# A kernel ordered by a planner: other DMA landings, margins and plays in the plan of attention with two gated layers

## The chip, the cores and the metric

The kernel runs on one core of a Trainium2 chip. The metric is the device time of one execution in microseconds; less is better. Beside the runs that were only timed there is one execution that the hardware profiler recorded, and every row below comes from that one.

## What is computed

Attention in chunks of 64 tokens (8 heads of 64, 4608 tokens), and then two layers on the 4608 x 512 result, the first with 1536 inner columns, the second with 2048. All is float32.

```python
scores = scale * np.matmul(q_c, k_c.transpose(0, 1, 2, 4, 3))
attn = np.exp(scores - np.max(scores, axis=-1, keepdims=True))
attn = attn / (np.sum(attn, axis=-1, keepdims=True) + 1e-09)
x = np.matmul(attn, v_c)                       # then as 4608 x 512
g = x @ w_gate
x = (g * (1.0 / (1.0 + np.exp(-g))) * (x @ w_val)) @ moe_w_out
h = x @ w_in
out = (h * (1.0 / (1.0 + np.exp(-1.702 * h)))) @ moe2_w_out
```

## The kernel before

**The work.** The tokens are cut into 9 blocks of 512 and the inner columns of each layer into two halves, so that there are four passes over the blocks: passes 0 and 1 for the first layer, 2 and 3 for the second. In pass 0 the attention of the next block is made between the products of the present one. Large products are made by a scheme of seven products of halves in place of eight (the labels 1 to 7), and each operand stands as a high and a low part, so that a product is three matmuls (L368 to L370, in `mm3`). A pass keeps its weights in SBUF; the tokens' combinations `x`, the output weights `o` and partial sums go through DRAM and come back by DMA.

**Weights of the next pass.** While a pass runs, the weights of the next one are prepared. `conv_tile` loads half a tile at a time into `raw` (two buffers, 255.8 KB each, L424) and `conv_part` takes it apart with two instructions on ACT (L447, L449) and two on DVE (L452, L455). POOL then makes the combinations and their low parts (L361, tiles `st` and `ws`), and SP stores them to DRAM (L348).

**The engines' queues.** Every engine works through its own list in order. All DMAs are issued by SP (L345 loads, L348 stores), so one that waits for its data holds up those behind it. ACT also copies products out of PSUM (`u<-ga`, L352, in `copy`), which sets the bank `ga` free for PE's next product.

**The planner.** The kernel lists its operations with a cost in us, the tiles they read and write, and a due time written by hand (`prio`); `Program` then sets the order in which they are written to the engines' lists, and only that order reaches the chip. `order` (L114) is a list scheduler: it lets each engine take, among the operations that are ready within a short window, the one with the earliest due time. For a DMA it supposes 1.5 us to the start, 0.865 of the cost for the transfer, behind the transfers before it, and 1.3 us to the landing. An operation of PE counts as ready `SLACK` (0.5 us) after its last operand, unless it brings a margin `near` of its own. `dues` (L160) works back from the end to the time by which each operation is due; `replay` (L186) plays the four engines and the DMA queue with the order fixed, with a model of PE's clock, and gives the time at the end. `emit` (L236) does this 12 times, each time with the due times halfway between the old and those of `dues`, and keeps the order whose replay ends first. `op` (L87) collects the dependencies; a tile that takes the place of an older one in its ring waits for the users of the older one that were listed by then (L98).

Of the kernel before, what the change touches and what calls it, by code (L numbers as in the profile page):

```python
# [2 lines left out]

# [24 lines left out]
class Buf:  # L28
# [2 lines left out]

    def __init__(self, make, prev=None, before=None, whole=None):
        self.make, self.prev, self.before, self.whole, self.bank = make, prev, before, whole, False
        self.users, self.writers, self.tile = [], [], None

    @property
    def ap(self):
# [15 lines left out]
class Ring:  # L53
# [5 lines left out]
    def new(self, shape, dtype=F32):  # L59
        def make():  # L60
            return self.pool.tile(shape, dtype, tag=self.tag, name=self.tag, bufs=self.bufs)

        prev = self.made[-self.bufs] if len(self.made) >= self.bufs else None
        b = Buf(make, prev, self.made[-1] if self.made else None)
        b.bank = self.pool is self.banks
        self.made.append(b)
        return b

# [6 lines left out]
class Program:  # L75
    HOP = {("pe", "dve"): 0.32, ("pe", "act"): 0.32, ("pe", "dma"): 0.3}
    WINDOW = {"pe": 0.3, "dve": 0.1, "act": 0.3, "pool": 0.3, "dma": 0.0}
    FREE = {"pe": 1.3, "pool": 0.7, "dma": 0.7, "act": 0.0, "dve": 0.0}
    SLACK = 0.5
    LOAD = 1.28  # L80
    ROUNDS = 12
    BEAT = 3.413
# [4 lines left out]
    def op(self, eng, us, fn, reads=(), writes=(), prio=0, table=None, near=None, port=None):  # L87
        o = Op()
        o.eng, o.us, o.fn, o.prio, o.table, o.near, o.n = eng, us, fn, prio, table, near, len(self.ops)
        o.port = eng == "pool" or eng == "dve" and port is not False and not any(a.bank for b in reads for a in b.line())  # L90
        deps, follows = set(), set()
        for b in reads:
            deps.update(next((a.writers for a in b.line() if a.writers), ()))
        for b in writes:
            deps.update(b.users)
            if not b.users:
                if b.prev is not None:
                    deps.update(b.prev.users)  # L98
                if b.before is not None and b.before.tile is None:
                    follows.add(b.before.users[0])  # L100
        for b in (*reads, *writes):
            for a in b.line():
                a.users.append(o)
        for b in writes:
            for a in b.line():
                a.writers.append(o)
        o.deps, o.follows = deps, follows - deps
        self.ops.append(o)
        return o
# [4 lines left out]
    def order(self):  # L114
        ready = {eng: [] for eng in self.FREE}
        for o in self.ops:
            o.ready, o.left = 0.0, len(o.deps) + len(o.follows)
            if not o.left:
                ready[o.eng].append(o)
        free, table, port, moved, seq = dict(self.FREE), None, 0.0, 0.0, []  # L120
        while len(seq) < len(self.ops):
            pick = None
            for eng, todo in ready.items():
                if not todo:
                    continue
                t = free[eng]
                limit = min(max(t, o.ready) for o in todo) + self.WINDOW[eng]
                o = min((o for o in todo if o.ready <= limit), key=lambda o: (o.key, o.n))
                s = max(t, o.ready)
                if pick is None or s < pick[0]:  # L130
                    pick = s, o
            s, o = pick
            ready[o.eng].remove(o)
            o.begin = s
            if o.eng == "dma":
                free["dma"] = s + 0.47
                moved = max(s + 1.5, moved) + 0.865 * o.us
                o.end = moved + 1.3
            else:
                if o.table and o.table != table:  # L140
                    s, table = s + self.LOAD, o.table
                if o.port:
                    o.end = max(s + 0.1, port) + o.us - 0.1
                    port = o.end - 0.1
                else:
                    o.end = s + o.us
                free[o.eng] = o.end - (0.05 if o.eng != "pe" else 0.0)
            seq.append(o)
            for a in o.after:
                if o in a.deps:  # L150
                    late = self.hop(o, a)
                    if a.eng == "pe" != o.eng:
                        late += self.SLACK if a.near is None else a.near
                    a.ready = max(a.ready, o.end + late)
                a.left -= 1
                if not a.left:
                    ready[a.eng].append(a)
        return seq

    def dues(self, seq):  # L160
        last = max(o.end for o in seq)
        for o in seq:
            o.left = len(o.after)
        heap = [(-o.end, -o.n, o) for o in seq if not o.left]
        heapq.heapify(heap)
        free = last
        while heap:
            o = heapq.heappop(heap)[2]
            t = last
            for a in o.after:  # L170
                if o not in a.deps:
                    t = min(t, a.due)
                else:
                    t = min(t, a.due - self.hop(o, a) - (self.SLACK if a.eng == "pe" != o.eng else 0.0))
            if o.eng == "dma":
                o.due = t - 2.8 - 0.865 * o.us
            elif o.eng == "pe":
                o.due = free = min(t, free) - o.us
            else:
                o.due = t - o.us  # L180
            for d in (*o.deps, *o.follows):
                d.left -= 1
                if not d.left:
                    heapq.heappush(heap, (-d.end, -d.n, d))

    def replay(self, seq):  # L186
        queue = {eng: [] for eng in self.FREE}
        for o in reversed(seq):
            queue[o.eng].append(o)
            o.end = None  # L190
        free, table, port, moved = dict(self.FREE), None, 0.0, 0.0
        busy, clock, beat = {}, 0.5, 0
        left, last = len(seq), 0.0
        while left:
            pick = None
            for eng, todo in queue.items():
                if not todo or any(d.end is None for d in todo[-1].deps):
                    continue
                o = todo[-1]
                s = max([free[eng], *(d.end + self.hop(d, o) for d in o.deps)])  # L200
                if pick is None or s < pick[0]:
                    pick = s, o
            s, o = pick
            queue[o.eng].pop()
            left -= 1
            us = o.us
            if o.eng == "dma":
                free["dma"] = s + 0.47
                moved = max(s + 1.5, moved) + 0.865 * us
                o.end = moved + 1.3  # L210
                continue
            if o.eng == "pe":
                while beat < s // self.BEAT:
                    share = busy.get(beat, 0.0) / self.BEAT
                    clock = 1.0 if share > 0.85 else 0.5 if share < 0.5 else clock
                    beat += 1
                if clock < 1.0 and us < 3.0:
                    us *= 1.8
                t = s
                while t < s + us:  # L220
                    k = t // self.BEAT
                    e = min(s + us, (k + 1) * self.BEAT)
                    busy[k] = busy.get(k, 0.0) + e - t
                    t = e + 1e-9
            if o.table and o.table != table:
                s, table = s + self.LOAD, o.table
            if o.port:
                o.end = max(s + 0.1, port) + us - 0.1
                port = o.end - 0.1
            else:  # L230
                o.end = s + us
            free[o.eng] = o.end - (0.05 if o.eng != "pe" else 0.0)
            last = max(last, o.end)
        return last

    def emit(self):  # L236
# [6 lines left out]
        for i in range(self.ROUNDS):  # L243
            seq = self.order()
            self.dues(seq)
            last = self.replay(seq)
            if best is None or last < best[0]:
                best = last, seq
            for o in self.ops:
                if o.prio < 9999:  # L250
                    o.key = (o.key + o.due) / 2
# [5 lines left out]
def attention_two_moe_kernel(ctx: ExitStack, tc: tile.TileContext, q, k, v, wg, wv, wo, wi, wo2, out):  # L257
# [38 lines left out]
    UPB = BT // P  # L296
# [744 lines left out]
    for p, (layer, gs) in enumerate(passes):  # L1041
        jobs = spread(p)
        for b in range(NB):
            t = start[p][b]
            xs = X.pop((p, b))
            for j, g in enumerate(gs):
# [62 lines left out]
                if p == 0 and b + 1 < NB:  # L1109
                    units = range(2 if b > 1 else 0, UPB + 2 if b else UPB)  # L1110
                    for u in units[len(units) * j // len(gs):len(units) * (j + 1) // len(gs)]:
                        if b:
                            attend_next(UPB * (b + 1) + u, t + -6.0 + (u - 2) * 13.5)
                        else:
                            attend(UPB + u, t + 4 + u * 16, t - 6 + u * 16)
                    if end:
# [54 lines left out]
```

## Time and profile before

| what | us |
|---|---|
| median of 3 runs | 1768.72 (1765.05 to 1769.85) |
| the profiled execution | 1770.99 |
| its span, from the first to the last instruction | 1769.2 |
| PE, matmuls busy in the span | 1704.2 |
| DVE, ACT, POOL busy | 1134.3, 888.1, 728.6 |

The span is read by engine and by stage. PE is the tensor engine's matmuls and PEld its weight loads, which run beside them; a matmul's end is modelled, so the idle time of PE comes out shorter than that of PEld. A wait is put down to what came last before the instruction could start. SPq is SP's queue of DMA issues.

### The profile page before, as it was taken

Reading aid. Unit: us, or ns where it says so; the run is one execution under the profiler, and the core shown is the slowest. Engines: PE = TensorE matmul, PEld = TensorE weight load, DVE = VectorE, ACT = ScalarE, POOL = GpSimd, SP = SyncE. Lnnn points to the kernel's source line nnn. Section 1 sums busy time; section 2 is a strip of 40 time slices with the busy share of each in tenths; the row PEclk is TensorE's granted clock in tenths of the full one; section 3 lists DMA queues with packets and bytes.
Section 4 is the critical chain, followed back from the end, with each engine's and each line's share of the span. In section 5 each row is a group of like instructions: output and inputs, shape, how many; then the busy total and the mean of one; then the engine's idle time right before and its main releaser. Section 6 shows DMA issues by size and latency. Waiting matters only on the chain.

```text
span 1769.2 us, 36486 instructions
## 1 busy us (share of the span) xinstructions
PE 1704.2 (96%) x14392; PEld 1618.5 (91%) x14392; DVE 1134.3 (64%) x1632; ACT 888.1 (50%) x1537; POOL 728.6 (41%) x762
## 2 busy tenths in 40 slices
PE   6899999999999999999999989999999999999998
PEld 6788889889889999999999889999999999999998
DVE  7887787778774345455444457777655556666656
ACT  6777666767653233333333345555544444444443
POOL 5754476666674011222212234757621133333333
PEclk7899999999999999999999999999999999999999
DMA  7468888888879767777778978988877977777783
GB/s 262 162 236 287 300 307 305 264 321 310 274 258 393 279 216 247 239 248 248 257 246 307 403 251 290 297 307 305 300 229 270 379 235 246 249 225 236 227 261 127
DMA packets 187323, 477.91 MB, mean 270 GB/s; under 512 B 20112, under 2 KB 47760, under 8 KB 187152
## 3 DMA queue, kind: packets, MB, share of 16 engines
q1 hardware_dynamic: 187152, 475.58, 78.2%
q8 instruction: 114, 1.87, 0.4%
q14 instruction: 57, 0.47, 0.1%
HBM read 334.46 MB, written 141.03 MB: 269 GB/s over the span
## 4 chain that ended last, share of the span: by engine, by line
PE 67%; DMA 13%; DVE 7%; POOL 5%; issue 4%; ACT 3%; SPq 0%; POOLq 0%; DVEq 0%; ACTq 0%
PE ga L368 8%; PE ga L370 8%; PE ga L369 8%; PE ya L368 4%; PE ya L370 4%; PE yb L368 4%; PE ya L369 4%; PE yb L370 3%; PE yb L369 3%; PE gb L368 3%; PE gb L370 3%; PE gb L369 3%; DMA raw<-in_moe_w_out 2%; PE s L368 2%; PE s L370 2%
## 5 line engine op out<-in xcount | busy, mean ns | idle before, releaser
L368 PE MATMUL ga<-x,w 128*128 128x256 f32 x1640 | 470.0, 287 | 20.9 <-ACT u L352 13.4
L369 PE MATMUL ga<-x,w 128*128 128x256 f32 x1640 | 464.6, 283 | 1.7 <-DVE x L361 1.7
L370 PE MATMUL ga<-x,w 128*128 128x256 f32 x1640 | 465.1, 284 | 0.7 <-POOL w L361 0.7
L368 PEld LDWEIGHTS ga<-x,w 128*128 128x128 f32 x1640 | 312.1, 190 | 37.0 <-ACT u L352 19.6
L369 PEld LDWEIGHTS ga<-x,w 128*128 128x128 f32 x1640 | 311.5, 190 | 7.7 <-DVE x L361 2.2
L370 PEld LDWEIGHTS ga<-x,w 128*128 128x128 f32 x1640 | 311.6, 190 | 0.9 <-POOL w L361 0.9
L352 ACT COPY u<-ga 128x512 f32<-128x512 f32 x231 | 134.7, 583 | 202.0 <-PE ga L370 201.6
L361 DVE TENSOR_TENSOR c<-u,ga 128x512 f32<-128x512 f32 x143 | 97.8, 684 | 129.7 <-PE ga L370 114.6
L361 POOL TENSOR_TENSOR k<-xr,q 128x512 fp32r<-128x512 f32 x24 | 34.3, 1427 | 329.1 <-DVE c L361 233.6
L361 DVE TENSOR_TENSOR c<-u,gb 128x512 f32<-128x512 f32 x125 | 85.3, 682 | 118.2 <-ACT u L352 103.2
L828 ACT ACTIVATE xr<-c 128x512 f32<-128x512 f32 x140 | 88.3, 631 | 142.0 <-DVE c L361 127.1
L368 PE MATMUL gb<-x,w 128*128 128x256 f32 x500 | 144.7, 289 | 7.1 <-DVE c L361 5.1
L369 PE MATMUL gb<-x,w 128*128 128x256 f32 x500 | 142.9, 286 | 3.1 <-POOL x L361 3.1
L370 PE MATMUL gb<-x,w 128*128 128x256 f32 x500 | 142.8, 286 | 0.0
L361 DVE TENSOR_TENSOR xr<-xr 128x512 f32<-128x512 f32 x140 | 123.3, 881 | 17.2 <-ACT xr L828 12.3
L788 ACT ACTIVATE h<-c 128x512 f32<-128x512 f32 x108 | 67.8, 631 | 102.7 <-DVE c L361 100.4
L361 DVE TENSOR_TENSOR h<-h,c 128x512 f32<-128x512 f32 x108 | 98.5, 920 | 27.4 <-ACT h L788 26.0
L361 POOL TENSOR_TENSOR u<-u 128x512 f32<-128x512 f32 x36 | 47.4, 1316 | 158.5 <-ACT u L352 158.5
L368 PEld LDWEIGHTS gb<-x,w 128*128 128x128 f32 x500 | 96.3, 193 | 12.6 <-DVE c L361 7.0
L447 ACT ACTIVATE t<-raw,offset 128x256 f32<-128x256 int16 x120 | 63.0, 527 | 87.4 <-DMA raw<-in_moe_w_out 31.1
L452 DVE SCALAR_TENSOR_TENSOR t<-t,raw 128x256 int32<-128x256 f32 x120 | 74.6, 628 | 48.0 <-ACT raw L449 41.7
L369 PEld LDWEIGHTS gb<-x,w 128*128 128x128 f32 x500 | 96.2, 192 | 6.7 <-POOL x L361 3.4
(252 smaller groups left out, 5003.4 us busy)
## 6 DMA issues: line engine op xcount, KB each, us to landing
x<-x_dram SPq DMA_DIRECT2D x189, 512.0 KB, 5.4
o<-od_b SPq DMA_DIRECT2D x119, 512.0 KB, 4.5
o<-od_a SPq DMA_DIRECT2D x102, 512.0 KB, 5.3
x_dram<-x SPq DMA_DIRECT2D x63, 512.0 KB, 5.3
wd_b<-ws SPq DMA_DIRECT2D x56, 256.0 KB, 4.2
od_b<-ws SPq DMA_DIRECT2D x56, 256.0 KB, 4.5
w<-wd_b SPq DMA_DIRECT2D x28, 512.0 KB, 6.4
raw<-in_moe_w_out SPq DMA_DIRECT2D x56, 255.8 KB, 4.2
```

What stands on the lines that cost most here:

```text
L352: op("act", act_us(n), lambda: nc.scalar.copy(out=dst.ap, in_=cut(src.ap)), [src], [dst], prio, near=near)
L361: lambda: e.tensor_tensor(out=dst.ap, in0=of_a(a.ap), in1=of_b(b.ap), op=by), [a, b], [dst], prio, near=near)
L368: nc.tensor.matmul(o, ah, bh, start=first, stop=False, **kind)
L369: nc.tensor.matmul(o, ah, bl, start=False, stop=False, **kind)
L370: nc.tensor.matmul(o, al, bh, start=False, stop=last, **kind)
L447: op("act", conv_us(n), lambda: nc.scalar.activation(out=t.ap, in_=raw.ap[:, :, 2], func=AF.Relu, scale=up, bias=offset.ap[:, :1]), [raw, ...
L452: op("dve", dve_us(n), lambda: nc.vector.scalar_tensor_tensor(out=t.ap.bitcast(I32), in0=t.ap, scalar=-4096 * up, in1=word(1).bitcast(F32) ...
L788: op("act", act_us(512), lambda h=h, i=i: nc.scalar.activation(out=h.ap, in_=of(0)(c[i].ap), func=AF.Silu), [c[i]], [h], prio, "silu")
L828: op("act", act_us(512), lambda: nc.scalar.activation(out=h.ap, in_=c.ap, func=AF.Gelu_apprx_sigmoid), [c], [h], prio, "gelu")
```

## The change

No instruction of the kernel is added or taken away; what is changed is what the planner supposes, and so the order of each engine's list.

- The landing of a DMA is supposed later: 0.95 of the cost in place of 0.865, and 2.4 us behind it in place of 1.3 (`LAND`). In the replay the part behind the transfer is 1.4 us with a scatter drawn anew for every DMA, and the time of an order is the mean of three such plays.
- `SLACK` goes from 0.5 to 0.3 us. Each step back from one operation to the one it needs takes 0.3 us more (`DUE`), and a DMA is due earlier by 0.7 us and the longer transfer.
- A tile that opens a reused place in a ring now depends on all users of the older tile, those listed later too (`openers`, `next`).
- The attention of blocks 2 and on gets other due times (L1113).

```diff
--- before.py
+++ after.py
@@ -1,4 +1,5 @@
 import heapq
+import random
 from contextlib import ExitStack
 
 import concourse.bass as bass
@@ -31,7 +32,7 @@
 
     def __init__(self, make, prev=None, before=None, whole=None):
         self.make, self.prev, self.before, self.whole, self.bank = make, prev, before, whole, False
-        self.users, self.writers, self.tile = [], [], None
+        self.users, self.writers, self.openers, self.next, self.tile = [], [], [], None, None
 
     @property
     def ap(self):
@@ -63,6 +64,8 @@
         prev = self.made[-self.bufs] if len(self.made) >= self.bufs else None
         b = Buf(make, prev, self.made[-1] if self.made else None)
         b.bank = self.pool is self.banks
+        if prev is not None:
+            prev.next = b
         self.made.append(b)
         return b
 
@@ -76,7 +79,9 @@
     HOP = {("pe", "dve"): 0.32, ("pe", "act"): 0.32, ("pe", "dma"): 0.3}
     WINDOW = {"pe": 0.3, "dve": 0.1, "act": 0.3, "pool": 0.3, "dma": 0.0}
     FREE = {"pe": 1.3, "pool": 0.7, "dma": 0.7, "act": 0.0, "dve": 0.0}
-    SLACK = 0.5
+    SLACK = 0.3
+    LAND = 2.4
+    DUE = 0.3
     LOAD = 1.28
     ROUNDS = 12
     BEAT = 3.413
@@ -96,11 +101,15 @@
             if not b.users:
                 if b.prev is not None:
                     deps.update(b.prev.users)
+                    list(b.line())[-1].openers.append(o)
                 if b.before is not None and b.before.tile is None:
                     follows.add(b.before.users[0])
         for b in (*reads, *writes):
             for a in b.line():
                 a.users.append(o)
+                for w in a.next.openers if a.next is not None else ():
+                    w.deps.add(o)
+                    w.follows.discard(o)
         for b in writes:
             for a in b.line():
                 a.writers.append(o)
@@ -134,8 +143,8 @@
             o.begin = s
             if o.eng == "dma":
                 free["dma"] = s + 0.47
-                moved = max(s + 1.5, moved) + 0.865 * o.us
-                o.end = moved + 1.3
+                moved = max(s + 1.5, moved) + 0.95 * o.us
+                o.end = moved + self.LAND
             else:
                 if o.table and o.table != table:
                     s, table = s + self.LOAD, o.table
@@ -171,9 +180,9 @@
                 if o not in a.deps:
                     t = min(t, a.due)
                 else:
-                    t = min(t, a.due - self.hop(o, a) - (self.SLACK if a.eng == "pe" != o.eng else 0.0))
+                    t = min(t, a.due - self.hop(o, a) - self.DUE - (self.SLACK if a.eng == "pe" != o.eng else 0.0))
             if o.eng == "dma":
-                o.due = t - 2.8 - 0.865 * o.us
+                o.due = t - 3.5 - 0.95 * o.us
             elif o.eng == "pe":
                 o.due = free = min(t, free) - o.us
             else:
@@ -183,7 +192,8 @@
                 if not d.left:
                     heapq.heappush(heap, (-d.end, -d.n, d))
 
-    def replay(self, seq):
+    def replay(self, seq, seed):
+        jitter = random.Random(seed)
         queue = {eng: [] for eng in self.FREE}
         for o in reversed(seq):
             queue[o.eng].append(o)
@@ -206,8 +216,8 @@
             us = o.us
             if o.eng == "dma":
                 free["dma"] = s + 0.47
-                moved = max(s + 1.5, moved) + 0.865 * us
-                o.end = moved + 1.3
+                moved = max(s + 1.5, moved) + 0.95 * us
+                o.end = moved + 1.4 + max(-1.2, jitter.gauss(0, 0.8))
                 continue
             if o.eng == "pe":
                 while beat < s // self.BEAT:
@@ -243,7 +253,7 @@
         for i in range(self.ROUNDS):
             seq = self.order()
             self.dues(seq)
-            last = self.replay(seq)
+            last = sum(self.replay(seq, j) for j in range(3)) / 3
             if best is None or last < best[0]:
                 best = last, seq
             for o in self.ops:
@@ -1110,7 +1120,7 @@
                     units = range(2 if b > 1 else 0, UPB + 2 if b else UPB)
                     for u in units[len(units) * j // len(gs):len(units) * (j + 1) // len(gs)]:
                         if b:
-                            attend_next(UPB * (b + 1) + u, t + -6.0 + (u - 2) * 13.5)
+                            attend_next(UPB * (b + 1) + u, t + -10.0 + (u - 2) * 14.5)
                         else:
                             attend(UPB + u, t + 4 + u * 16, t - 6 + u * 16)
                     if end:
```

## Rows read from the trace of the kernel before

**Rows 1.** The page, part 1: PE's busy time, share and instructions.
```profile
PE 1704.2 (96%) x14392; PEld 1618.5 (91%) x14392; DVE 1134.3 (64%) x1632; ACT 888.1 (50%) x1537; POOL 728.6 (41%) x762
```

**Rows 2.** Windows: busy PE, PEld, DVE, ACT, POOL (count), PEclk, DMA share, GB/s.
```profile
0.00:100.00 100.00, 76.53 (x822) 67.90 (x823) 79.72 (x116) 69.45 (x133) 65.14 (x77) 0.80 0.60 211
100.00:560.00 460.00, 444.42 (x4428) 406.11 (x4427) 360.58 (x550) 300.27 (x515) 282.04 (x336) 1.00 0.84 294
560.00:985.00 425.00, 425.00 (x2950) 396.51 (x2949) 206.28 (x283) 142.01 (x244) 77.01 (x55) 1.00 0.76 263
985.00:1080.00 95.00, 87.61 (x632) 82.70 (x631) 53.51 (x77) 45.46 (x78) 23.73 (x18) 0.95 0.85 311
1080.00:1290.00 210.00, 199.66 (x1617) 195.13 (x1616) 148.02 (x214) 113.85 (x205) 139.58 (x173) 0.99 0.90 302
1290.00:1740.00 450.00, 448.45 (x3765) 447.78 (x3764) 269.96 (x373) 209.07 (x351) 133.04 (x99) 1.00 0.77 255
```

**Rows 3.** Waits of PEld, 100 to 560 us: total, times, longest.
```profile
PEld ga L368 <- ACT u L352: 14.3, 11, 3.1
PEld gb L368 <- DVE c L361: 3.0, 6, 0.9
```

**Rows 4.** Timeline of PE at five places: start, length, instruction [idle before <- releaser].
```profile
153.11 0.39 PE L368 MATMUL ga<-x,w 128*128 128x256 f32 x1 [1.05 <-ACT u L352]
...
212.07 0.39 PE L368 MATMUL ga<-x,w 128*128 128x256 f32 x1 [1.47 <-ACT u L352]
...
272.48 0.39 PE L368 MATMUL ga<-x,w 128*128 128x256 f32 x1 [0.79 <-ACT u L352]
...
333.10 0.39 PE L368 MATMUL ga<-x,w 128*128 128x256 f32 x1 [1.91 <-ACT u L352]
...
453.38 0.39 PE L368 MATMUL ga<-x,w 128*128 128x256 f32 x1 [2.71 <-ACT u L352]
```

**Rows 5.** Timeline of ACT ahead of the last of these five.
```profile
450.81 0.52 ACT L447 ACTIVATE t<-raw,offset 128x256 f32<-128x256 int16 x1 [4.45 <-DMA raw<-in_moe_w_in]
...
452.76 0.57 ACT L352 COPY u<-ga 128x512 f32<-128x512 f32 x1
```

**Rows 6.** The tile raw, 100 to 560 us: who waited for it (us, times); landing.
```profile
  ACT t L447: 43.3, 21
...
DMA to landing us min/median/max: 2.5/4.2/7.7
```

**Rows 7.** DMA issues of the whole run: count, KB each, median us to landing.
```profile
o<-od_b SPq DMA_DIRECT2D x119, 512.0 KB, 4.5
```

**Rows 8.** Waits of PEld, 1080 to 1290 us: total, times, longest.
```profile
PEld ya L368 <- ACT hh L352: 1.9, 2, 1.4
...
PEld s L368 <- DMA o<-od_b: 1.6, 2, 0.9
PEld yb L368 <- DMA o<-od_b: 1.6, 1, 1.6
PEld ya L368 <- ACT e L352: 1.2, 1, 1.2
PEld a L368 <- DMA o<-od_b: 1.2, 2, 0.8
```

**Rows 9.** Timeline of ACT ahead of the longest wait for hh of rows 8.
```profile
1263.81 0.53 ACT L447 ACTIVATE t<-raw,offset 128x256 f32<-128x256 int16 x1 [3.34 <-DMA raw<-in_moe_w_out]
```

**Rows 10.** Windows of 25 us after two of these stalls; columns as in rows 2.
```profile
450.00:475.00 25.00, 22.29 (x193) 20.38 (x193) 19.39 (x26) 16.75 (x30) 17.64 (x22) 0.93 0.72 239
...
1250.00:1275.00 25.00, 22.83 (x176) 22.22 (x175) 16.48 (x22) 12.41 (x22) 18.70 (x23) 0.93 0.82 275
```

**Rows 11.** Window of 25 us in the opening; columns as in rows 2.
```profile
25.00:50.00 25.00, 16.36 (x141) 14.61 (x142) 23.38 (x25) 17.68 (x34) 23.57 (x22) 0.53 0.50 178
```

**Rows 12.** Waits of SP's queue, 100 to 560 us: total, times, longest.
```profile
SPq L348 <- POOL ws L361: 71.2, 56, 3.4
SPq L345 <- DVE t L455: 53.3, 36, 4.3
```

## The prediction, made before the result was known

> **What bounds the kernel now.** I read the page first: PE's matmuls are busy in 1704.2 us of the span of 1769.2, so at most 65 us are lost on PE by that row [rows 1]. The windows say where. From 560 to 985 us PE is never idle. The idle time lies in the opening (100 - 76.53 = 23.5 us), in pass 0 from 100 to 560 us (460 - 444.42 = 15.6), at the change from the first layer to the second (7.4) and in pass 2 from 1080 to 1290 us (10.3) [rows 2]. Pass 0 and that part of pass 2 are where the next pass's weights are loaded, taken apart and stored again: DMA share 0.84 and 0.90 there, POOL busy 282 of 460 and 140 of 210 us [rows 2].
>
> Then the waits, stage by stage. In pass 0 the largest is that of PE for the copy that empties the bank ga: 14.3 us in 11 waits [rows 3]. I went to the longer ones in the timeline, and at five of them the same picture stands on ACT ahead of the copy: PE is idle for 1.05, 1.47, 0.79, 1.91 and 2.71 us, 7.9 together [rows 4]. At the last of the five, ACT sat idle for 4.45 us at L447 until a half tile of raw had landed, did the conversion, and reached the copy u<-ga at 452.76 [rows 5]. The bank had been full long before; the copy stood behind an instruction that waited for a DMA. The other four have the same wait at L447 one to five places ahead of the copy. Over pass 0, L447 waited for raw 43.3 us in 21 times [rows 6].
>
> **Why the planner put it there.** It supposes that a lone half tile (cost 0.74) lands 1.5 + 0.865 x 0.74 + 1.3 = 3.44 us after its issue. In pass 0 the trace has 2.5 / 4.2 / 7.7 us (least, median, most) [rows 6]. More than half land later than the plan, and the order of ACT's list is made from the plan. For a load of 512 KB (cost 1.48) it supposes 4.08 us; the o tiles of the second layer take 4.5 in the median [rows 7], and PE waits for them itself in pass 2: 1.6 + 1.6 + 1.2 = 4.4 us in five waits [rows 8].
>
> **The change part by part.** The changed plan supposes 1.5 + 0.95 x 0.74 + 2.4 = 4.60 us for the half tile, 1.16 more, and 5.31 for 512 KB, 1.23 more. No instruction and no DMA is added; what I cost is what the new order does to each wait.
>
> *Copies behind L447 in pass 0.* If the conversion stands 1.16 us later in ACT's list, each of the five stalls shrinks by at most that much, or vanishes where the copy now goes ahead. The smaller count is 1.05 + 1.16 + 0.79 + 1.16 + 1.16 = 5.3 us; the larger is all 7.9; the lower end is nothing. I take 5.3, as the stalls beyond 1.16 us come from landings that are later than the new plan too. What is late next there is DVE's sum (6 waits, 3.0 us [rows 3]). The conversions move, and with them DVE's L452 and L455, POOL's combinations and the stores on SP. SP's queue already waits 71.2 us for POOL's ws and 53.3 us for L455 to free a raw buffer [rows 12]; loads behind these stores are issued later. I cost this at nothing, since the two largest waits of PE here are for ACT and DVE and not for a DMA [rows 3]; without that cover, the loads of o and x pay.
>
> *PE's own wait for o in pass 2.* Five waits, the longest in the largest row 1.6 us. With 1.23 us more allowed each, 4.4 - (1.6 - 1.23) = 4.0 us go. Ends: 0 and 4.4.
>
> *The second layer's hh and e.* PE waits 1.9 us in 2 and 1.2 us in 1 for tiles that ACT makes [rows 8]; ahead of the longest for hh (1.4), ACT had sat 3.34 us at L447 [rows 9], and the one for e has the same. Two times 1.16: 2.3 us. Ends: 0 and 2.6.
>
> *The clock.* After the stalls at 453 and 1266 us a piece at the lower of the two levels (1.2 of 2.4 GHz) follows: the mean granted clock of the two windows is 0.93 [rows 10], so each costs 0.07 x 25 = 1.75 us. PE had idled in the stretch before it. If the stalls shrink, either may go: 0 to 3.5 us; I take one, 1.75.
>
> *Smaller SLACK, and DUE.* PE's operations may stand 0.2 us closer to their operands. Of the waits on ACT and DVE in pass 0 there are 11 + 6 = 17 in these rows [rows 3]; if each grew by the whole 0.2, 3.4 us. The nearest row on the other side is pass 1, where no idle shows at all [rows 2]. I take 2.0 us as a loss. The DUE term moves all due times the same way; I cost it with this one.
>
> *The opening.* DVE and POOL are busy in 23.4 and 23.6 of 25 us from 25 to 50 us [rows 11]; another order cannot make their work less. I take 0, with -5 to +5 us (about a fifth of the 23.5 idle) as ends, since the first loads are put in another order too.
>
> *All users of a reused place.* This adds edges in the plan. The chip waited for these places before, so it costs nothing there; in the second layer after 1290 us PE idles for only 450 - 448.45 us anyway [rows 2]. Taken as 0; at most those 1.5 us gain. The attention's due times move by 1 to 4 us and its loads with them: 0, covered by the products that PE has ready in pass 0; the end on either side lies within the opening's 5. The plays choose among 12 orders that differ; I take the gain from them as held in the terms above.
>
> *Sum.* 5.3 + 4.0 + 2.3 + 1.75 - 2.0 = 11.35 us less. The profiled execution took 1770.99 us (its span 1769.2 and 1.8 around it), which gives 1759.6. It lies 2.27 us above the median of 1768.72, so I forecast 1757.4.
>
> **A rule that speaks against it.** The half tile's median of 4.2 us is the number on which the first term rests [rows 6]; the row's least, 2.5 us, is shorter than even the old plan. The Trainium skill (DMA: Bandwidth & Descriptors, section on the anatomy of one DMA) gives a fit of about 2.0 us plus the bytes over 436 GB/s, measured on another issuing path than SP's; for 255.8 KB that is an estimate of 2.6 us. By that rule the old plan would already be too cautious and the change would gain nothing; the trace agrees with it only for its fastest landing.
>
> **The rivals.**
> *No change.* The landing is late by accident, not by a constant: from 2.5 to 7.7 us [rows 6], and a plan that allows 4.60 is still wrong for the tail, while the conversions that are put off hold raw longer. Then the five stalls in pass 0 reappear elsewhere, half of the o term (2.0 us) is gained, the SLACK term (2.0) eats it, and the time is 1768.7. For it: the longest stall, 2.71 us, came from a wait of 4.45 us, far over 1.16. Against: the stalls gather where conversions and copies share a queue and are absent in pass 1. That the plan changes but the order does hardly, so that the change does not do what it says, ends at the same time. The fit of the Trainium skill named above would lead to this time too.
> *Slower.* The smaller SLACK decides: PE's list puts a product 0.2 us nearer to its operand, and where ACT or DVE are late by some tenths, PE stalls, in the full passes too. By the kernel's costs a step of the first layer (7 products of 1.427 us, 8 of 0.695) is 15.55 us with 15 operations; from 100 to 1740 us there are some 1580. If 8 in 100 lose 0.2 us, that is 25 us against 13.35 gained: 1768.7 + 12 = 1781. It decides from 6 in 100 on ((13.35 + 5.3) / 0.2 = 93 operations). Against it: pass 1 has no idle time at all with 0.5 [rows 2], so there is room.
> *A larger gain.* The copies go ahead of the conversions altogether, and the chosen order is good against scatter in general: 7.9 + 4.4 + 2.6, both pieces of low clock 3.5, half of the other waits for u ((14.3 - 7.9) / 2 = 3.2), 5 in the opening, no loss by SLACK: 26.6 us, 1742.
>
> **How the numbers follow.** The forecast 0.58, the larger gain 0.12, no change 0.19, slower 0.11. A measurement of this kernel can tell a difference of about 0.3%, 5.3 us. So faster by more 0.70 (the first two), within 0.19, slower 0.11. The range goes from the larger gain, 1742, to no change with a bad opening, 1768.7 + 5 = 1773.7, say 1774; it leaves out the slower case and little beyond the larger gain.
>
> **What would show it.** Right: in pass 0 the total that L447 waits for raw falls well below 43.3 us, PEld's wait for u from 14.3 to under 9, the o waits of pass 2 almost go, and one of the two clock dips does. Pass 1 and the second half of the second layer stay without idle time. Wrong: L447 still waits some 40 us for raw and PE for u (no change); many short waits on ACT and DVE in the stretches from 560 to 985 and from 1290 us (slower); or the gain lies in the opening, which I cost at nothing.

## The result: a gain of 41 us, and the profile after

The changed kernel takes 1728.52 us in the median against 1769.28 for the kernel before: a ratio of 0.9766, 95% interval 0.9734 to 0.9799. The forecast was 1757.4 with a range of 1742 to 1774. The direction was right, the size, 11 us, was little more than a quarter of the measured one, and the range missed. Ratios compare fast executions; one slow one, of the kernel all_but_land below (3294.97 us), stands in none of them.

The page of the changed kernel, its span and part 1 (busy time). Its line numbers are 10 higher than those of the kernel before: L368 is L378 here, L447 is L457.

```profile
span 1726.9 us, 36534 instructions
...
PE 1687.4 (98%) x14392; PEld 1609.8 (93%) x14392; DVE 1125.8 (65%) x1632; ACT 902.0 (52%) x1545; POOL 732.0 (42%) x762
```

The same 14392 matmuls are done [rows 1]; their busy time falls by 17 us, of the 42 by which the span is shorter; the other 25 us are idle time that is gone. Some 8 of the 17 us are pieces at the lower clock level that are gone (counted below, at the clock); these rows don't show what the rest is. The same stretches as in [rows 2]:

```profile
0.00:100.00 100.00, 77.56 (x865) 71.45 (x866) 77.86 (x123) 74.09 (x145) 67.51 (x80) 0.83 0.60 211
100.00:560.00 460.00, 459.04 (x4565) 423.46 (x4564) 358.68 (x553) 313.58 (x521) 260.30 (x305) 1.00 0.88 306
560.00:985.00 425.00, 425.00 (x2942) 395.54 (x2941) 210.09 (x287) 146.57 (x253) 93.01 (x86) 1.00 0.78 276
985.00:1080.00 95.00, 89.22 (x714) 86.19 (x713) 65.34 (x91) 53.45 (x94) 42.41 (x38) 1.00 0.80 285
1080.00:1290.00 210.00, 208.16 (x1726) 205.83 (x1725) 160.20 (x223) 115.74 (x206) 131.88 (x156) 1.00 0.90 305
```

From 100 to 560 us PE is idle for 1.0 us where it had been idle for 15.6, and its clock is at the upper level from 100 to 1290 us, where the stretch from 985 to 1080 had a mean of 0.95. Fixed stretches hold other work once a kernel is faster, so where the time was gained is read from places that both kernels share. The last product of attention with v ends pass 0's attention. Before and after, in the views of L591 and L601:

```profile
L591 PE MATMUL a<-e,v x1056: 218/218/367, 16.3 to 523.2; 64*64 64x64 f32 x176
```

```profile
L601 PE MATMUL a<-e,v x1056: 217/218/364, 21.2 to 497.3; 64*64 64x64 f32 x176
```

It starts 25.9 us earlier. The windows up to these two moments, before and after, show that as much work was done by then, 5000 and 4997 matmuls:

```profile
0.00:523.20 523.20, 485.29 (x5000) 441.19 (x5002) 417.87 (x640) 355.33 (x623) 324.35 (x389) 0.96 0.79 276
```

```profile
0.00:497.30 497.30, 474.54 (x4997) 437.34 (x4999) 400.05 (x626) 359.98 (x615) 298.95 (x352) 0.97 0.81 279
```

The first store of the final output starts at 1398.5 instead of 1440.9, so another 16.5 us are gained in between; the last store of the same tile starts at 1722.3 instead of 1764.6, so nothing is gained behind:

```profile
L348 SPq DMA_DIRECT2D out<-yv x18: 372/389/1193, 1440.9 to 1764.6; - x18
```

```profile
L358 SPq DMA_DIRECT2D out<-yv x18: 372/388/673, 1398.5 to 1722.3; - x18
```

Windows that begin at 0 count the matmuls started: 8195, 8826 and 10441 of them by 985, 1080 and 1290 us in the kernel before. The changed kernel has as many 25, 31 and 43 us earlier. So pass 0 with the opening gave 25 us, pass 1 nothing, the change of layers 6, that part of pass 2 some 12, and the last pass nothing. Pass 0 and pass 2 are where the weights of the next pass are prepared.

The waits of PEld from 100 to 560 us, against [rows 3]:

```profile
PEld a L601 <- issue: 5.1, 14, 0.4
PEld gb L378 <- DVE c L371: 1.1, 2, 0.8
...
PEld ga L378 <- ACT u L362: 0.3, 1, 0.3
```

PE's wait for the copy out of the bank ga went from 14.3 us in 11 waits to 0.3 us in one. The other side of this is in ACT's own waits in the same stretch (one row of that view before, two after):

```profile
ACT u L352 <- PE ga L370: 26.3, 23, 3.6
```

```profile
ACT u L362 <- PE ga L380: 59.1, 40, 5.1
...
ACT t L457 <- DMA raw<-in_moe_w_out: 5.2, 5, 1.7
```

In the kernel before, ACT waited at this copy for PE 26.3 us in 23 times; now 59.1 us in 40. The copy stands in the list early enough for ACT to wait for the bank, and PE hardly waits for ACT any more. A piece of ACT's timeline shows one such place:

```profile
430.85 0.59 ACT L362 COPY u<-ga 128x512 f32<-128x512 f32 x1 [0.52 <-PE ga L380]
432.81 0.53 ACT L457 ACTIVATE t<-raw,offset 128x256 f32<-128x256 int16 x1 [1.37 <-DMA raw<-in_moe_w_out]
```

ACT still waits for raw, but behind the copy: [rows 5] had the two the other way round. In the view of the tile raw from 100 to 560 us:

```profile
  ACT t L457: 9.3, 12
...
DMA to landing us min/median/max: 2.5/4.3/8.9
```

The landings are what they were (2.5 / 4.2 / 7.7 in [rows 6]); ACT's wait for them fell from 43.3 to 9.3 us. The DMAs did not become faster; the lists came to expect them.

### The profile page after: what moved, and what is told of

The parts are those of the page before. It is cut to its first block, busy times and chain, and to the rows that moved or that the text cites. A ratio compares the mean times of both kernels' runs of the same rounds, so it can differ in the third digit from the quotient of the medians.

```text
span 1726.9 us, 36534 instructions
## 1 busy us (share of the span) xinstructions
PE 1687.4 (98%) x14392; PEld 1609.8 (93%) x14392; DVE 1125.8 (65%) x1632; ACT 902.0 (52%) x1545; POOL 732.0 (42%) x762
## 3 DMA queue, kind: packets, MB, share of 16 engines
q8 instruction: 113, 1.85, 0.4%
## 4 chain that ended last, share of the span: by engine, by line
PE 86%; POOL 3%; DVE 3%; issue 3%; ACT 2%; DMA 2%; SPq 0%; POOLq 0%; DVEq 0%; ACTq 0%
PE ga L378 10%; PE ga L380 10%; PE ga L379 10%; PE ya L378 5%; PE ya L379 5%; PE ya L380 4%; PE yb L378 4%; PE yb L380 4%; PE yb L379 4%; PE gb L378 4%; PE gb L380 4%; PE gb L379 4%; PE s L378 2%; PE s L380 2%; PE s L379 2%
## 5 line engine op out<-in xcount | busy, mean ns | idle before, releaser
L378 PE MATMUL ga<-x,w 128*128 128x256 f32 x1640 | 467.4, 285 | 6.7 <-DVE c L371 2.9
L378 PEld LDWEIGHTS ga<-x,w 128*128 128x128 f32 x1640 | 310.2, 189 | 18.1 <-DVE c L371 4.4
L371 POOL TENSOR_TENSOR u<-u 128x512 f32<-128x512 f32 x36 | 52.4, 1455 | 238.0 <-ACT u L362 238.0
L378 PE MATMUL gb<-x,w 128*128 128x256 f32 x500 | 143.1, 286 | 0.8 <-DVE c L371 0.8
L371 DVE TENSOR_TENSOR xr<-xr 128x512 f32<-128x512 f32 x140 | 110.5, 790 | 15.9 <-ACT xr L838 10.3
L798 ACT ACTIVATE h<-c 128x512 f32<-128x512 f32 x108 | 67.9, 632 | 100.9 <-DVE c L371 98.8
L371 DVE TENSOR_TENSOR hl<-xr,hh 128x512 fp32r<-128x512 f32 x70 | 53.8, 768 | 79.1 <-ACT hh L362 79.1
L371 DVE TENSOR_TENSOR h<-h,c 128x512 f32<-128x512 f32 x108 | 86.3, 806 | 28.4 <-ACT h L798 26.5
L371 DVE TENSOR_TENSOR hl<-h,hh 128x512 fp32r<-128x512 f32 x108 | 86.9, 807 | 22.1 <-ACT hh L362 20.2
L378 PEld LDWEIGHTS gb<-x,w 128*128 128x128 f32 x500 | 95.3, 191 | 5.5 <-DVE c L371 1.8
```

Of the source, the lines that this page charges most:

```text
L371: lambda: e.tensor_tensor(out=dst.ap, in0=of_a(a.ap), in1=of_b(b.ap), op=by), [a, b], [dst], prio, near=near)
L378: nc.tensor.matmul(o, ah, bh, start=first, stop=False, **kind)
L798: op("act", act_us(512), lambda h=h, i=i: nc.scalar.activation(out=h.ap, in_=of(0)(c[i].ap), func=AF.Silu), [c[i]], [h], prio, "silu")
```

## The experiments

Eighteen kernels were run, each three rounds against the kernel before. Their theories: L, that the supposed landings decide; P, that the choice by plays does; R, that any other order falls where it falls. The last two columns of this table are from the trace, 100 to 560 us: ACT's wait for raw in all, and PEld's wait for the copy u out of ga. "Gain" is one minus the ratio, times 1768 us.

| kernel | ratio, 95% interval | gain us | ACT for raw | PEld for u |
|---|---|---|---|---|
| the change | 0.9766, 0.9734 to 0.9799 | 41 | 9.3 | 0.3 |
| users_only | 1.0010, 0.9995 to 1.0026 | -2 | 48.1 | 17.2 |
| land_users | 0.9803, 0.9789 to 0.9818 | 35 | 8.1 | 0.8 |
| all_but_land | 1.0020, 1.0005 to 1.0034 | -4 | 47.7 | 15.2 |
| all_but_plays | 0.9802, 0.9787 to 0.9816 | 35 | 7.1 | 0.5 |
| land_raw | 0.9908, 0.9874 to 0.9943 | 16 | 32.7 | 7.5 |
| land_rest | 0.9853, 0.9824 to 0.9881 | 26 | 12.8 | 2.5 |
| land_185 | 0.9813, 0.9784 to 0.9842 | 33 | 15.0 | 5.8 |
| land_35 | 0.9806, 0.9777 to 0.9835 | 34 | 4.8 | 2.7 |
| land_stores | 0.9846, 0.9825 to 0.9867 | 27 | 36.2 | 6.8 |
| land_loads | 0.9926, 0.9911 to 0.9941 | 13 | 44.0 | 10.7 |
| order_half | 0.9792, 0.9775 to 0.9810 | 37 | 3.3 | 0.9 |
| dues_half | 0.9984, 0.9966 to 1.0001 | 3 | 45.4 | 11.4 |
| land_ws | 0.9931, 0.9911 to 0.9951 | 12 | 49.1 | 11.8 |
| land_other | 0.9888, 0.9861 to 0.9915 | 20 | 49.4 | 10.4 |
| raw_stores | 0.9766, 0.9741 to 0.9790 | 41 | 12.7 | none |
| all_but_margins | 0.9774, 0.9755 to 0.9792 | 40 | 8.9 | 0.4 |
| tail_only | 0.9807, 0.9790 to 0.9823 | 34 | 30.2 | 2.3 |
| rate_only | 0.9887, 0.9871 to 0.9904 | 20 | 25.5 | 5.6 |

### Which part of the change

**users_only**: before, plus `openers` and `next` as in the diff above, nothing else.

> The kernel before with one part of the change alone: a reused place waits in the plan for all users of the older tile. Theory L (the supposed landings decide): no gain, 1763 to 1775 us, with L447 in pass 0 still waiting some 40 us for raw. Theory P (the choice by scattered plays decides): the same, 1763 to 1775. Theory R (any other order falls where it falls, some 40 us wide): a time that is off by more than 8 us either way, with the wait of L447 changed at random.

Measured 1766.89 us. No gain, and by its interval hardly any difference; R's kind of jump did not come.

**land_users**: users_only, and

```diff
-                moved = max(s + 1.5, moved) + 0.865 * o.us
-                o.end = moved + 1.3
+                moved = max(s + 1.5, moved) + 0.95 * o.us
+                o.end = moved + 2.4
-                o.due = t - 2.8 - 0.865 * o.us
+                o.due = t - 3.5 - 0.95 * o.us
```

and in the replay 0.95 and 1.4, without scatter.

> Two parts alone: the later landings in order, due times and replay (replay at their mean, without scatter), and the known users. SLACK 0.5, no DUE, the old due times of attention. Theory L: at least 25 of the 41 us, so 1744 us or less, and L447 waits under 20 us for raw in pass 0. Theory P: a gain of under 12 us, above 1757. Theory R: no connection between the wait of L447 and the time.

Measured 1730.56 us. **all_but_land** is the changed kernel with these lines of `order` and `dues` put back:

> The changed kernel with the old supposition in order and due times (1.3 us behind 0.865 of the cost, due 2.8 earlier); the plays, SLACK, DUE, users and attention as changed. Theory L: loses at least 20 us, 1749 or more, L447 back at over 30 us for raw in pass 0. Theory P: stays within 8 us of the changed kernel, under 1737. Theory R: anything from 1720 to 1770.

Measured 1770.69 us. **all_but_plays** takes out the scatter alone:

```diff
-                o.end = moved + 1.4 + max(-1.2, jitter.gauss(0, 0.8))
+                o.end = moved + 1.4
```

> The changed kernel with the scatter taken out of the replay: three equal plays at the mean landing. Theory L: within 6 us of the changed kernel, 1723 to 1735. Theory P: loses at least 15 us, 1743 or more. Theory R: off by more than 8 us as soon as another of the 12 orders is chosen.

Measured 1729.82 us. **all_but_margins** puts back `SLACK = 0.5` and takes the 0.3 of `DUE` away:

> The changed kernel with SLACK 0.5 and DUE 0 as before. If the smaller margin costs PE small stalls, as the prediction's sum had it (2 us): 2 us faster than the changed kernel, 1724 to 1728. If the parts of the change do nothing beside the landings: 1726 to 1733. If they carry a gain of their own: 1734 or more.

Measured 1729.56 us, a ratio of 0.9774, which can't be told from the change. So L holds and P and R fall: every kernel with the later landings in the list scheduler for all DMAs lies within 1728 to 1733 us, however its order was chosen, and the three without them in it lie at 1766 to 1771. The attention's due times had no run of their own; they belong to what the change has beyond land_users, 6 us by the ratios, with intervals that overlap.

The later landings without the part on users were not tried on the chip: there the planner may list a write into a place ahead of an older tile's last use, since it knows of no edge between them, and the engines' lists would wait for each other. That part is worth no time by itself; how far it is what makes the rest possible stays open.

### Order or due times, and how much

**order_half** has the old `o.due = t - 2.8 - 0.865 * o.us`, **dues_half** the old two lines in `order`; the rest is as changed.

> The changed kernel with the later landing in the list scheduler alone; the due times use the old 2.8 us and 0.865. If the order of each list follows from when an operation counts as ready: within 6 us of the changed kernel, 1723 to 1735. If from the due times: 1750 or more.

> The changed kernel with the later landing in the due times alone (DMAs due earlier); the list scheduler supposes the old one. If readiness decides: little gained, 1755 to 1772, with L447 waiting over 30 us for raw in pass 0. If earlier due times are enough, since they issue the loads sooner: 1723 to 1740.

Measured 1730.69 and 1765.94 us, with ACT waiting 45.4 us for raw in dues_half. What decides is the time from which an operation counts as ready in `order`, and not the due times; by the code, that time bears on who is ahead of whom in each list.

**land_185** and **land_35** have `LAND = 1.85` and `LAND = 3.5` in place of 2.4.

> The changed kernel with LAND at 1.85 us in place of 2.4, half way from the old 1.3 (a lone half tile is then supposed to land after 4.05 us, a little under the measured median of 4.2). If each us of allowance takes away a us of each stall, about half of the gain: 1745 to 1752. If what counts is whether the copies stand ahead of the conversions, and the median is enough for that: within 6 us of the changed kernel, 1724 to 1736.

> The changed kernel with LAND at 3.5 us (a lone half tile after 5.70 us, later than three quarters of the landings). If allowance is a cost once it exceeds the landing (raw's two buffers are held longer, conversions come later): slower than the changed kernel by over 5 us, 1734 or more. If it is free as long as other work fills the engines: 1722 to 1733, with L447's wait for raw under 5 us in pass 0.

Measured 1732.66 and 1731.49 us, both in the range of the second expectation. But land_185 keeps the longer transfer, which with `LAND` at the old 1.3 gains 20 us by itself (rate_only, below). With that transfer the gain at 1.3, 1.85, 2.4 and 3.5 us of `LAND` is 20, 33, 41 and 34 us: half of the step to 2.4 brings 13 of 21 us. So this run doesn't refute the first expectation, that the gain grows with the allowance; its range had left the transfer's part out. With 3.5 us the median is 3 us above the changed kernel's; by the ratios it is 7 us, with intervals that overlap. An allowance that is too long cost little here, if anything.

**tail_only** has 0.865 in `order` with `LAND` at 2.4; **rate_only** has 0.95 with `LAND = 1.3`.

> The changed kernel with the old 0.865 of the cost for the transfer in the list scheduler; LAND 2.4 stays. If the time behind the transfer is what counts: within 8 us of the changed kernel, 1722 to 1737. If the transfers' queue counts: 1750 or more. If each gives its part: 1737 to 1750.

> The changed kernel with LAND at the old 1.3 in the list scheduler; 0.95 of the cost for the transfer stays. If the time behind the transfer counts: 1755 or more, with L447 waiting over 30 us for raw in pass 0. If the transfers' queue counts: 1722 to 1737. If each gives its part: 1737 to 1755.

Measured 1732.13 and 1746.41 us. The time behind the transfer alone gives 34 us, as the first expectation of tail_only has it, and the longer transfer alone 20, in the range in which each gives its part. They don't add: together they gain 41. For a lone half tile the longer transfer is only 0.06 us more; in the plan transfers stand behind one another, so it adds up where they queue.

### Which DMAs

All of these start from users_only and use the later landing for one class of DMAs, in `order`, `dues` and replay. A mark is set where the DMA is listed (`"raw"` for the half tiles, `"store"` or `"ws"` for stores), and

```diff
+                late = o.table == "raw"
+                moved = max(s + 1.5, moved) + (0.95 if late else 0.865) * o.us
+                o.end = moved + (2.4 if late else 1.3)
```

with other conditions for the others. **land_raw** and **land_rest** first:

> Known users, and the later landing supposed for the loads of raw alone (120 half tiles); all other DMAs as before. Theory A (the stalls come from conversions placed ahead of their raw tile): over two thirds of the gain of all landings, 1730 to 1743 us, L447 waits under 15 us for raw in pass 0. Theory B (it is the whole of the DMAs: x, o, w, stores and attention's loads count at least as much): 1748 or more, with L447's wait gone all the same.

> Known users, and the later landing supposed for every DMA but the loads of raw. Theory A: a gain of at most 12 us, 1754 to 1768, from PE's own waits for o and the change of layers; L447 still waits some 40 us for raw in pass 0. Theory B: 1730 to 1748.

Measured 1748.87 and 1739.82 us. Theory A is the one of the prediction, and it falls in its narrow form: raw alone gives 16 us, everything but raw 26, and the latter even takes ACT's wait for raw from 48.1 (users_only) to 12.8 us, although the plan still lets raw land early. Theory B has both times in its ranges, but not its condition: in land_raw ACT's wait for raw is not gone, 32.7 us of it are left.

**land_stores** and **land_loads** split the rest:

> Known users, and the later landing supposed for stores alone. All DMAs but raw gave 26 us. Theory S (a store that lands late keeps POOL off its ws buffer, POOL keeps SP's next store waiting, and the raw loads behind it on SP are issued late): most of that, 1740 to 1750 us, L447's wait in pass 0 under 20 us, SP's wait for POOL's ws less than before. Theory B (the other loads: o, attention's tiles): under 8 us gained, 1758 or more.

> Known users, and the later landing supposed for all loads but raw. Theory S: under 10 us gained, 1756 or more, with PE's waits for o in pass 2 gone. Theory B: 1740 to 1750.

Measured 1740.34 and 1755.32 us. With the other loads alone PE's waits for o in pass 2 are gone, as expected; the 13 us gained lie between the two expectations, S's less than 10 and B's 1740 to 1750 us. Stores alone give 27 us, as S had it, but not by S's road: ACT still waits 36.2 us for raw, where S had under 20. What fell is PE's wait for u, from 17.2 us (users_only) to 6.8. That row of PEld's waits in land_stores, 100 to 560 us:

```profile
PEld ga L379 <- ACT u L363: 6.8, 5, 1.9
```

SP's waits for POOL's ws there fell as S expected, from 71.2 [rows 12] and 33.0 us. The second row of the kernel before, and then both in land_stores:

```profile
SPq L348 <- POOL ws L354: 33.0, 17, 3.6
```

```profile
SPq L358 <- POOL ws L372: 57.3, 47, 4.6
...
SPq L358 <- POOL ws L365: 8.8, 9, 3.7
```

**land_ws** is the stores that read ws, the prepared weights; **land_other** is the other stores. Of the two theories named there, Pace has the slower weight preparation as the cause, and read-back the other stores, whose data come back by a load:

> Known users, and the later landing supposed for the stores of prepared weights alone (those that read ws). Pace: at least two thirds of the 28 us of all stores, 1738 to 1751 us, and fewer ws stores issued by the time PE has done the same work in pass 0. Read-back: under 8 us gained, 1759 or more.

> Known users, and the later landing supposed for all stores but those of ws. Pace: under 9 us gained, 1757 or more. Read-back: 1738 to 1750.

Measured 1757.72 and 1748.64 us. In land_ws the weight preparation is indeed slower: 98 stores of ws from 100 to 560 us against 108 in the kernel before, and 108 in land_other. Yet land_ws gains the less. Pace as the cause falls. Read-back has land_other's 1748.64 in the range that it gave, but land_ws gained 12 us where it had under 8, between the two expectations, and no run here shows which reader it would be.

**raw_stores** takes the half tiles and all stores together:

> Known users, and the later landing supposed for raw's loads and all stores, that is for the loop of the weight preparation at both its ends; the loads of x, o, w and attention as before. If the loop is the whole effect: within 6 us of all landings together, 1725 to 1737. If the two are separate and add: 17 + 28 us gained, 1720 to 1726. If other loads are needed: 1738 to 1746.

Measured 1729.01 us, the whole gain, in the range of the first expectation. But the set is more than the loop of the weight preparation, as which the expectation has it: the stores of land_other are in it. The classes do not add: 16, 12, 20 and 13 us (raw, ws, other stores, other loads) are 61 us alone, and no kernel gained more than 41. Why the other stores give more than those of ws is left open. What the table shows is that PE's wait for u goes with the time: 10.4 us or more in six of the eight kernels that gain 20 us or less (7.5 and 5.6 in land_raw and rate_only), 6.8 or less in all that gain 26 or more. None of the eighteen is clearly faster than the changed kernel; raw_stores and all_but_margins equal it.

## Why the prediction was wrong, by its own steps

**What bounds the kernel.** Right in the main: most of the loss lay in pass 0 and pass 2, the copy u behind the conversion was its chief form, and the plan's early landings were the reason. Every sign listed for being right came. The amount that could be won was read too small, because it went by the idle time of PE, 15.6 us in pass 0. By PEld an estimate is 23.1 us: pass 1, with no stall, has PEld at 396.51 of 425 us, 93.3%; 93.3% of 460 is 429.2, and pass 0 had 406.11 [rows 2]. (Pass 0 has the attention's small products too, so its own ceiling may be another; no run shows it.) The Trainium skill has a rule on this (Perfetto Trace Analysis, the section on identifying the most-contended engine): for TensorE the busy share of matmuls is a poor measure of the distance to the limit, and the weight loads' share is one of the two to use. The trace agrees: of the 25.9 us gained up to pass 0's last attention, PEld has 22.0 as idle time that is gone (82.0 to 60.0 us in the two windows from 0), PE 15.1 (37.9 to 22.8).

**Copies behind L447 in pass 0** is the step that failed: "each of the five stalls shrinks by at most that much". I let a later landing of 1.16 us take at most 1.16 us from a stall and got 5.3 us. The step had the other case too, that a stall "vanishes where the copy now goes ahead", with 7.9 for all five; I set it aside because the stalls beyond 1.16 us come from landings that are later than the new plan too. Measured, PEld's wait for the copy went from 14.3 to 0.3 us, so the term is 14.0. The cap was wrong: the longest wait was 3.1 us, and it went like the others, while raw's landings stayed as late as they were (4.2 and 4.3 us in the median) and ACT's wait for raw fell from 43.3 to 9.3. Once the copy stands ahead of the conversion, its wait for that conversion is gone whole. Two smaller faults add to it. I measured the five stalls by PE's idle time, 7.9 us; PEld waits 10.1 us at the same five places (1.47, 1.90, 1.21, 2.34 and 3.14 in its timeline). And the six other waits, 4.2 us by PEld, went too. Waits of PEld for DVE's c in pass 0, which no term priced, shrank beside it: 2.7 us for ga to none, 3.0 for gb to 1.1. The larger gain's "half of the other waits" took PE's 7.9 from PEld's 14.3 and so mixed the two.

**Terms at nothing.** The prediction put the stores on SP at nothing, as a possible loss, because the two largest waits of PE are for ACT and DVE. That the plan's landing of a store is itself changed had no term; later landings of stores alone give 27 us. In the plan a DMA that ends later keeps its buffer and what reads its data waiting, and with a longer transfer also the DMAs behind it, so it can move work of other engines; which of these ways the gain of the stores takes is open. The change of layers, named with 7.4 us of idle time, had no term either, and gave 6 us, most of them by the clock (below). In pass 2 three waits were priced, and that part gained 12 us; PEld's wait for hl, 2.5 us in 3 in the view of rows 8, was not priced, and it is gone too.

**PE's own wait for o in pass 2**: forecast 4.0 us of 4.4. The waits of PEld from 1060 to 1290 us in the changed kernel have these rows for o and e:

```profile
PEld gb L378 <- DMA o<-od_b: 0.5, 1, 0.5
PEld ya L378 <- ACT e L362: 0.3, 1, 0.3
```

So 3.9 us went. The number is right, but it doesn't bear out the cap: all but one of these waits were shorter than 1.23 us, so the cap hardly came into it. **hh and e**: 2.3 forecast with 2.6 as the end; hh is gone from that view and 0.3 us for e is left, so 2.8 of 3.1 us went, again more than the cap allowed.

**The clock**: I took one dip of two. Both went, and with them two more at the change of layers that I had not counted (a granted clock of 0.66 from 1010 to 1015 us and of 0.56 from 1055 to 1060): 0.05 x 95 = 4.75 us by the mean of 0.95 there [rows 2]. PE still idles in that stretch, 5.8 us where it had been 7.4, and yet no piece at the lower level follows; why is open.

**Smaller SLACK**: forecast a loss of 2.0 us. all_but_margins gives 40 us of gain against 41 with it, and the intervals overlap: no loss is seen, and one of 2 us is too small to be told here. **The opening**: 0 forecast with 5 as its end. PEld does 71.45 us of work in the first 100 instead of 67.90, so it gained some 4 us, inside the ends. **All users**: 0 forecast, no gain measured. **The plays**: held in the other terms; 1729.82 without them.

**The fit from the Trainium skill** that would have made the old plan too cautious (DMA: Bandwidth & Descriptors, the section on the anatomy of one DMA; an estimate of 2.6 us for the half tile) is not borne out by what the change did. The trace has 2.5 us as the landing's least, but a median of 4.2, and supposing 4.05 us (land_185) and 4.60 us (the change) gained 33 and 41 us.

**The rivals.** No change, slower by SLACK: neither came. The larger gain, at 0.12 and 1742, was the nearest: it had the copies ahead of the conversions altogether, which is what happened in the main, and the range ended there because I summed only the waits that I had found a name for. Its 26.6 us held 5 in the opening and nothing for the change of layers.

## What to carry to other kernels

Where a planner fixes each engine's order, its guess of a DMA's landing helps to decide who stands ahead of whom. Moving an instruction that waits can take away the stall behind it whole, so price such a change by the whole of the stalls behind the waiting instruction, not by the difference of the guesses. Guess late rather than early, and for stores as well as loads: with the longer transfer, 1.85 to 3.5 us behind it gained between 33 and 41 us here and 1.3 us gained 20; with the old transfer, 1.3 us is the kernel before. Estimate the amount that can be won from the weight loads, against a stretch of the same kernel that has no stall.

## What was not expected

ACT's wait for raw was a good sign of the fault and a poor measure of its cost: tail_only has 30.2 us of it with 34 us gained, land_other 49.4 us with 20 gained. So the sum of these waits did not tell their cost; what stood behind them did, PE's wait for u above all (2.3 and 10.4 us). And a longer supposed transfer alone, 0.95 for 0.865 of the cost and no more behind it (rate_only), gave 20 us. The new order also has ACT load its tables more often, 26 and 25 times at L798 and L643 where the kernel before had 22 and 22, so 7 loads of 1.28 us more; ACT had room for these 9 us.
